# Batch 0's q and k in 128-token blocks, its first seven units one at a time, and half of the first MoE chunk in 512-token tiles

## The chip, the cores and the metric

The kernel runs on one core of one Trainium2 chip. The core has a matrix engine (TensorE, PE in the profile; its weight loads are listed apart as PEld), a vector engine (DVE), an activation engine (ACT), GpSimd (POOL) and SyncE (SP). SP, ACT and POOL also issue transfers to the core's 16 DMA engines. SBUF is the on-chip memory of 128 partitions; PSUM holds matmul results in eight banks of 128 x 512 float32. The metric is the device time of one execution in microseconds (us). Before the change the median of three runs is 310.25 us (309.75 to 310.46).

## The reference

Eight batches, eight heads, 576 tokens, head width 64. Attention has a sliding window of 128 tokens and a linear bias per head (ALiBi); its output, laid out as 4608 tokens by 512 features, goes through a two-matmul block with the activation h cos h.

```python
scores = scale * np.matmul(q, k.transpose(0, 1, 3, 2))
rel = pos[:, None] - pos[None, :]
mask = (rel >= 0) & (rel < window)                 # window = 128
scores = np.where(mask, scores + slopes * -abs(rel), -1e9)
attn = softmax(scores)                             # over keys
x = (attn @ v).transpose(0, 2, 1, 3).reshape(4608, 512)
h = x @ w_in                                       # 512 x 2048
out = (h * np.cos(h)) @ w_out                      # 2048 x 512
```

## The kernel before, in words

**Attention.** Queries of a batch come in five blocks of 128 tokens (the last has 64). The work is cut into units: unit (b, 0, 0) is block 0 with all eight heads; (b, qb, hh) for qb = 1 to 3 is a block with four heads; (b, 4, 0) is the 64-token tail with all heads. A unit computes `scores` (keys on the partitions, PE line 568, into two PSUM banks), an exponential on ACT over 128 x 1024 values (line 595), a multiplication by the mask on DVE (line 614; the first five units get bias and mask by a matmul into PSUM instead, line 582), the product with v (`pv`, PE lines 630 to 644; v has a column of ones for the sum), a division (`norm`, DVE lines 667 to 681), and a transposition of the result into the array `xT` (features on the partitions): by PE and a copy (`x_pe`, lines 702 to 731) or by DMA (`x_dma`).

**MoE.** Tokens go in nine chunks of 512. MoE1 makes 16 groups of 128 hidden features (fc 0 to 15) for a chunk, four matmuls each (one per 128 input features), then cos on ACT and a product on DVE into `gT`. From chunk 1 on a group is one PSUM bank of 128 features by 512 tokens (`moe1`, line 759, four matmuls of 512 columns). In chunk 0 `moe1_block` (line 784) fills a bank with four groups of features by 128 tokens, sixteen matmuls of 128 columns, so that it can start on tokens 0 to 127 before the later tokens exist. MoE2 (`moe2`, line 812) accumulates 16 matmuls of 512 columns per 128 tokens, copies the result and stores it.

**q and k.** Scores need q and k with head features on the partitions. Batches 2 to 7 are loaded in 128-token blocks into `qnat` and `knat` (`load_nat`, line 402) and transposed by DMA. Batches 0 and 1 are transposed by PE. They come as "rows": each partition takes several neighbouring tokens of one head, so a piece of memory read at once is 1 KB or more. Batch 0 is loaded in four such pieces (`PIECES`): tokens 0 to 127 (float32, by SP and ACT), 128 to 255, 256 to 511, and 512 to 575 (`qend`, `kend`); batch 1 in one. `qk_transposes` turns them: PE transposes of 128 x 64 into half of the partitions each (line 509, mode 2 of the planner; the first piece whole, line 504), then a copy out of PSUM by ACT or DVE (lines 524, 525) that also sorts the tokens. `tkeys` says which pieces a unit needs.

**Queues.** All loads but the first pieces go through POOL's queue in program order (lines 383, 391, 402, 423, 430): q and k pieces, v by 128-token block (`load_v`), w_in in five parts, w_out in four. The parts of w_in that chunk 0 waits for are called w0-1 (fc 0 and 1), w1-2 (fc 2 and 3), w2-4 (fc 4 to 7), w4-6 (fc 8 to 11), w6-8 (fc 12 to 15) here.

**The planner.** `Plan.op` records each operation with what it reads and writes, a cost and a priority; `Plan.schedule` orders them by a list schedule with those costs and emits the engines' programs with semaphore waits. On PE, operations of priority below 5 that can start at once go first; ties go by program order. All Sin activations of chunk 0 wait until the exponentials of the first seven units are done, since the activation table has to be switched. Until 8.3 us of plan time the planner fills PE's gaps with matmuls on zeros (line 945).

**Around the change.** `attention(every[0:7], -1)` runs units (0,0,0) to (0,3,1), which make tokens 0 to 511, in groups of two. Then comes chunk 0: `moe1_block` in the order (token block, group of four features) (0,0) (1,0) (2,0) (0,1) (1,1) (2,1) (3,0) (3,1), then groups 2 and 3 for the four token blocks; batch 1's row transposes come behind blocks 9 and 12. Chunk 0's MoE2 runs beside the attention of batch 1.

Of the kernel before, what the change touches and what calls it, by code (L numbers as in the profile page):

```python
# [6 lines left out]
ALU = mybir.AluOpType  # L7
ACTF = mybir.ActivationFunctionType
# [5 lines left out]
NBLK = 5  # L14
# [272 lines left out]
def bass_alibi_sliding__then__act_gcu_kernel(  # L287
# [8 lines left out]
    with ExitStack() as ctx:  # L296
# [13 lines left out]
        qE = {"q": sb("qend", [128, 2, 128]), "k": sb("kend", [128, 2, 128])}  # L310
# [51 lines left out]
        def piece_keys(which, b, n):  # L362
            return [("qB", which, i) for i in range(3)] if b else [("qB", which, n)]

        def load_qk(which, src, b, n=0):
            t0, rr, _ = PIECES[b][n]
            c0 = 64 * (t0 // 32)
            rows = bass.AP(src.tensor, src[b].offset + 64 * t0,
                           [[64 * rr, 32], [64 * S, H], [1, 64 * rr]])
            if b == 0 and n == 0:  # L370
# [8 lines left out]
                   r=[("qF", which)], w=piece_keys(which, b, n), occ={"act": 460, "dve": 330},  # L379
                   lat={"act": 560, "dve": 410}, pri=2)  # L380
                return
            o = qE[which][:, :, :] if t0 == 512 else qB[which][:, :, c0:c0 + 64 * rr]
            op("pool", [lambda e: e.dma_start(o, rows)],  # L383
               w=piece_keys(which, b, n), dma=f"ld{which}{n}", occ=750,
               lat={2: 600, 4: 800 if which == 'q' else 900,
                    8: 2600 if which == 'q' else 1300, 18: 2850}[rr])

        def load_v(b, order=range(NBLK), behind=()):
            for t in order:
# [6 lines left out]
                   occ=900, lat=7 * rows)  # L396

        def load_nat(which, src, b):
# [6 lines left out]
            op("pool", fns, w=[("nat", which)], dma=f"ldn{which}", occ=4400, lat=5500)  # L405
# [29 lines left out]
        def constants():  # L435
# [9 lines left out]
            for i, (edge, test) in enumerate([(-127.0, ALU.is_lt), (0.0, ALU.is_gt)]):  # L445
# [3 lines left out]
            op("dve", lambda e: e.tensor_tensor(dif[:, :, :], dif[:, :, :], off[:, :, :], ALU.add),  # L449
               r=[("off", 0), ("off", 1)], w=["dif"], occ=350, lat=430, pri=0)  # L450
            for i in range(2):
                op("dve", lambda e, i=i: e.memset(vp[i][:, :, :, 64:65], 1.0), w=[("vinit", i)],
                   pri=5 * i)
                op("dve", lambda e, i=i: e.memset(vp[i][64:128, 4, :, 0:64], 0.0),
                   w=[("vinit", i)], occ=270, pri=5 * i)
            for i in range(NP):
                op("dve", lambda e, i=i: e.memset(P[i][:, 1024:1088], 0.0), w=[("P", i)], occ=90)
            op("dve", lambda e: e.memset(halfpi[:, :], math.pi / 2.0), w=["halfpi"], occ=60)
# [28 lines left out]
        def qk_transposes(b, names, n, parts, banks):  # L487
# [8 lines left out]
            def dst(i):  # L496
                return ps[:, banks[i], :].bitcast(BF16)[:, 0:128 * (jobs[i][2] - jobs[i][1])]
# [479 lines left out]
```

## Time and profile before

| | |
|---|---|
| median of three runs | 310.25 us (309.75 to 310.46) |
| profiled execution, its own time | 310.24 us |
| span of the profile | 308.4 us |
| PE busy | 299.5 us (97%) |
| ACT busy | 200.3 us (65%) |
| DVE busy | 195.8 us (63%) |
| POOL busy | 97.0 us (31%) |
| granted PE clock | 1.00 in all windows |

The span lies inside the time of the execution; 1.84 us lie around it. An engine's busy time is the sum of its instructions; matmuls overlap in the records, so the pace of a group of matmuls is read from the distance between starts, or from the chain, which gives every stretch to one instruction only. A DMA row gives the time from the start of its issue to the landing of its last byte. KB are those written to SBUF (bf16), 1024 bytes each; GB/s of a window are bytes moved per time.

### The profile page before, as it was taken

How to read it: one execution, taken by the hardware profiler on the slowest of the kernel's cores; microseconds unless marked ns; L12 is line 12 of the kernel's file. 1: busy time of each engine (PE TensorE's matmuls, PEld its weight loads, DVE VectorE, ACT ScalarE, POOL GpSimd, SP SyncE). 2: the span in 40 equal slices, each digit the busy share in tenths (PEclk: the TensorE clock that was granted, in tenths of full speed). 3: DMA queues.
4: the chain of work that ended last, by engine and by line, in shares of the span. 5: the costliest groups of instructions: out<-in, count | busy, mean ns of one | idle time of the engine just before them, and what ended most of it. 6: DMA issues, size and time to landing. Idle time of an engine off the chain costs nothing.

```text
span 308.4 us, 6675 instructions
## 1 busy us (share of the span) xinstructions
PE 299.5 (97%) x2685; PEld 162.1 (53%) x2726; DVE 195.8 (63%) x409; ACT 200.3 (65%) x267; POOL 97.0 (31%) x122
## 2 busy tenths in 40 slices
PE   8889999999999999999999999999999999999996
PEld 6679755445554455445544554455445554444444
DVE  7688777574668566856785568656966588742000
ACT  6887973875478745873688378746964488752211
POOL 8997200455055505550347123900500000000000
PEclk9999999999999999999999999999999999999999
DMA  9999999999499958998699969995991420001112
GB/s 147 179 204 207 206 162 193 132 183 154 122 121 138 172 98 154 133 175 98 157 114 149 167 88 180 150 184 114 143 113 44 113 70 0 0 0 70 68 71 99
DMA packets 150333, 39.09 MB, mean 127 GB/s; under 512 B 138912, under 2 KB 145312, under 8 KB 150304
## 3 DMA queue, kind: packets, MB, share of 16 engines
q0 software_dynamic: 100688, 18.10, 79.5%
q1 hardware_dynamic: 49344, 20.33, 33.3%
q8 instruction: 21, 0.34, 0.5%
q10 hardware_dynamic: 272, 0.26, 0.3%
q14 instruction: 8, 0.07, 0.1%
HBM read 36.70 MB, written 9.44 MB: 150 GB/s over the span
## 4 chain that ended last, share of the span: by engine, by line
PE 90%; DMA 3%; POOL 2%; ACT 2%; issue 1%; DVE 1%; POOLq 0%; ACTq 0%
PE ps L812 38%; PE ps L759 36%; PE ps L568 5%; PE ps L784 4%; DMA w_inb<-in_moe_w_in_dram 3%; ACT p L595 2%; PE ps L642 2%; PE ps L644 2%; PE ps L630 1%; POOL vp L391 1%; PE ps L509 1%; DVE p L614 1%; PE ps L634 1%; POOL qrows L383 0%; PE ps L721 0%
## 5 line engine op out<-in xcount | busy, mean ns | idle before, releaser
L812 PE MATMUL ps<-w_outb,gT 128*128 128x512 bf16 (+2 forms) x566 | 132.1, 373 | 2.5 <-issue 1.3
L759 PE MATMUL ps<-xT,w_inb 128*128 128x512 bf16 x499 | 113.9, 379 | 0.7
L768 DVE TENSOR_TENSOR gT<-ps,cos 128x512 bf16<-128x512 f32 x128 | 85.1, 688 | 19.6 <-ACT cos L764 14.7
L764 ACT ACTIVATE cos<-ps,halfpi 128x512 f32<-128x512 f32 x128 | 84.6, 687 | 18.0 <-PE ps L759 13.9
L812 PEld LDWEIGHTS ps<-w_outb,gT 128*128 128x128 bf16 x592 | 53.4, 98 | 55.7 <-DVE ob L820 0.3
L595 ACT ACTIVATE p<-ps 128x1024 bf16<-128x1024 f32 x64 | 61.5, 1023 | 31.2 <-PE ps L568 31.0
L759 PEld LDWEIGHTS ps<-xT,w_inb 128*128 128x128 bf16 x512 | 49.0, 98 | 56.2 <-ACT p L595 0.6
L391 POOL DMA_DIRECT2D vp<-in_v_dram x40 | 33.7, 870 | 87.6 <-DMA xT<-xnat 67.4
L614 DVE TENSOR_TENSOR p<-p,emask 128x1024 bf16<-128x1024 bf16 x59 | 39.7, 684 | 27.8 <-ACT p L595 27.8
L819 ACT ACTIVATE ob<-ps 128x512 f32<-128x512 f32 (+2 forms) x21 | 12.1, 576 | 41.6 <-PE ps L812 35.2
L402 POOL DMA_DIRECT2D qnat<-in_q_dram x30 | 25.3, 877 | 22.5 <-DMA qt<-qnat 22.5
L402 POOL DMA_DIRECT2D knat<-in_k_dram x30 | 25.4, 884 | 12.3 <-DMA kt<-knat 9.8
L820 DVE COPY ob<-ps 128x512 f32<-128x512 f32 x16 | 11.0, 685 | 15.8 <-PE ps L812 15.7
L681 DVE TENSOR_TENSOR xnat<-ps,rec 128x256 bf16<-128x256 f32 x48 | 19.9, 421 | 1.3
L568 PE MATMUL ps<-qt,kt 64*128 64x128 bf16 (+1 forms) x576 | 19.4, 211 | 0.3 <-DVE qt L525 0.2
L642 PEld LDWEIGHTS ps<-vp,p 128*128 128x128 bf16 x192 | 14.2, 97 | 9.9 <-issue 6.4
L568 PEld LDWEIGHTS ps<-qt,kt 64*128 64x128 bf16 x576 | 14.5, 94 | 8.7 <-issue 3.5
L642 PE MATMUL ps<-vp,p 128*128 128x65 bf16 x192 | 17.4, 193 | 0.7 <-DVE xT L731 0.5
L644 PE MATMUL ps<-vp,p 128*128 128x65 bf16 x192 | 17.5, 193 | 0.0
L784 PE MATMUL ps<-xT,w_inb 128*128 128x128 bf16 x256 | 16.0, 219 | 0.6 <-DMA w_inb<-in_moe_w_in_dram 0.6
L784 PEld LDWEIGHTS ps<-xT,w_inb 128*128 128x128 bf16 x256 | 14.5, 98 | 1.3 <-DMA w_inb<-in_moe_w_in_dram 0.8
L644 PEld LDWEIGHTS ps<-vp,p 128*128 128x128 bf16 x192 | 13.2, 97 | 2.2
(66 smaller groups left out, 160.9 us busy)
## 6 DMA issues: line engine op xcount, KB each, us to landing
out_dram<-ob SPq DMA_DIRECT2D x35, 256.0 KB, 2.2
vp<-in_v_dram POOLq DMA_DIRECT2D x32, 128.0 KB, 7.1
qnat<-in_q_dram POOLq DMA_DIRECT2D x24, 128.0 KB, 6.5
knat<-in_k_dram POOLq DMA_DIRECT2D x24, 128.0 KB, 5.1
w_outb<-in_moe_w_out_dram POOLq DMA_DIRECT2D x4, 512.0 KB, 21.8
w_inb<-in_moe_w_in_dram POOLq DMA_DIRECT2D x3, 512.0 KB, 12.2
qrows<-in_q_dram POOLq DMA_DIRECT2D x1, 576.0 KB, 15.5
krows<-in_k_dram POOLq DMA_DIRECT2D x1, 576.0 KB, 17.5
```

Of the source, the lines that this page charges most:

```text
L391: op("pool", [lambda e, t=t, rows=rows: e.dma_start(vp[b % 2][0:rows, t, :, 0:64], v[b, :, 128 * t:128 * t + rows, :].rearrange("h p d -> ...
L402: fns.append(lambda e, t=t, rows=rows: e.dma_start(nat[which][0:rows, t, :, :], src[b, :, 128 * t:128 * t + rows, :].rearrange("h p d -> p ...
L568: ins = e.matmul(ps[:, banks[x], c0:c0 + n_], keys_ap(b, x, pr, kc), query_ap(b, x, pr, qb, n_), start=not acc, stop=stop)
L595: op("act", lambda e: e.activation(P[i][:, 0:1024], ps[:, banks[0]:banks[0] + 2, :].rearrange("p a b -> p (a b)"), ACTF.Exp, scale=0.125), ...
L614: op("dve", lambda e: e.tensor_tensor(p, p, m, ALU.mult), r=[("P", i), ("EM", 0), ("EM", 1)], w=[("P", i)], occ=600, lat=690, pri=1)
L642: e.matmul(o, P[i][:, c0:c0 + 128], V[:, qb - 1, h, 0:65], start=True, stop=False)
L644: ins = e.matmul(o, P[i][:, c0 + 128:c0 + 256], V[:, qb, h, 0:65], start=False, stop=True)
L759: op("pe", lambda e, kc=kc: e.matmul(ps[:, bank, :], w_in[:, kc, 128 * fc:128 * fc + 128], xT[:, kc, r0:r0 + CH], start=(kc == 0), stop=(k ...
L764: op("act", lambda e: e.activation(cosb[ci][:, :], ps[:, bank, :], ACTF.Sin, bias=halfpi[:, 0:1]), r=["halfpi"], w=[("B", bank), ("cos", c ...
L768: op("dve", lambda e: e.tensor_tensor(gT[gi][:, fc, :], ps[:, bank, :], cosb[ci][:, :], ALU.mult), r=[("cos", ci)], w=[("B", bank)] + [("g ...
L784: ins = e.matmul(ps[:, bank, 128 * i:128 * i + 128], w_in[:, kc, 128 * fc:128 * fc + 128], xT[:, kc, t0:t0 + 128], start=(kc == 0), stop=( ...
L812: op("pe", lambda e, t=t, fc=fc, bank=bank, j0=j0, j1=j1: e.matmul(ps[:, bank, 0:j1 - j0], gT[gi][:, fc, 128 * t:128 * t + 128], w_out[:, ...
```

## The change

Three things change, and with them some of the planner's numbers.

1. **q and k of batch 0 from token 128.** The pieces of rows go. Tokens 128 to 575 are loaded by `load_block` in 128-token blocks (t = 1 to 3; t = 4 has 64 tokens, its other rows are zeroed by DVE) into `qnat` and `knat`, in the layout of `load_nat`: one token per partition, 256 bytes read at once. `block_transposes` turns a block by four whole 128 x 128 transposes and one copy. A unit waits for its own blocks only (`tkeys`). The order of POOL's queue is written as a list: v3 moves behind w1-2, q3 and k3 lie behind w0-1. The first `load_nat` (batch 2) must wait until the blocks have been transposed. `qend` and `kend` go.
2. **The first seven units** are planned in groups of one, with the same two pairs of banks in turn.
3. **MoE1 of chunk 0, fc 8 to 15,** is done by `moe1` (four matmuls of 512 columns, all 512 tokens); fc 0 to 7 stay in blocks of 128 tokens. Batch 1's row transposes come behind tiles 10 and 13.

The initial values of the v buffers are set after the bias table's base is made; the planner's costs of a bias on DVE, of the first v block and of batch 1's rows are changed by some 50 to 500 ns.

```diff
-        PIECES = {0: [(0, 4, [(0, 4)]), (128, 4, [(0, 4)]), (256, 8, [(0, 4), (4, 8)]),
-                      (512, 2, [(0, 2)])],
-                  1: [(0, 18, [(0, 5), (5, 10), (10, 14), (14, 18)])]}
+        ROWS = [(4, [(0, 4)]), (18, [(0, 5), (5, 10), (10, 14), (14, 18)])]
...
+        def load_block(which, src, t):
+            rows = 128 if t < 4 else 64
+            op("pool", [lambda e: e.dma_start(
+                nat[which][0:rows, t, :, :],
+                src[0, :, 128 * t:128 * t + rows, :].rearrange("h p d -> p h d"))],
+               r=[("nend", which)] if t == 4 else [], w=[("nb", which, t)], dma=f"lb{which}{t}",
+               occ=900, lat=7 * rows)
...
-            op("pool", fns, w=[("nat", which)], dma=f"ldn{which}", occ=4400, lat=5500)
+            op("pool", fns, w=[("nat", which)] + [("nb", which, t) for t in range(1, NBLK)],
+               dma=f"ldn{which}", occ=4400, lat=5500)
...
+        def block_transposes(names, t, banks):
+            def f(e):
+                ins = None
+                for which, bank in zip(names, banks):
+                    for pr in range(NPAIR):
+                        ins = e.transpose(
+                            ps[:, bank, :].bitcast(BF16)[:, 128 * pr:128 * pr + 128],
+                            nat[which][:, t, 2 * pr:2 * pr + 2, :].rearrange("p h d -> p (h d)"),
+                            ident[:, :])
+                return ins
...
-            keys = [("tr", w_, b % 2) for w_ in ("q", "k")] + [("ktail", b % 2)]
-            if b < BPE:
-                lo, hi = 128 * max(0, qb - 1), 128 * qb + 128
-                keys += [("tr", w_, b % 2, t0 + j0) for w_ in ("q", "k")
-                         for t0, rr, groups in PIECES[b] if t0 < hi and t0 + 32 * rr > lo
-                         for j0, _ in groups]
+            keys = [("tr", w_, b % 2) for w_ in ("q", "k")]
+            if qb == 4 or b >= BPE:
+                keys += [("ktail", b % 2)]
+            if b == 0:
+                keys += [("tr", w_, 0, t) for w_ in ("q", "k") for t in range(max(0, qb - 1), qb + 1)]
...
-            sizes = ([[2] * 4] + GROUPS + [[], []])[phase + 1]
+            sizes = ([[1] * 7] + GROUPS + [[], []])[phase + 1]
...
-        load_qk("q", q, 0, 1)
-        load_qk("k", k, 0, 1)
-        load_v(0, [0])
-        load_qk("q", q, 0, 2)
-        load_qk("k", k, 0, 2)
-        load_v(0, [1])
-        load_w_in(0, 1)
-        load_v(0, [2, 3])
-        load_w_in(1, 2)
-        load_w_in(2, 4)
-        load_w_in(4, 6)
-        load_qk("q", q, 0, 3)
-        load_qk("k", k, 0, 3)
+        for x in "q1 k1 v0 q2 k2 v1 w0-1 q3 k3 v2 w1-2 v3 w2-4 w4-6 q4 k4 w6-8 qr kr v4".split():
...
+        for t in range(1, 4):
+            for which, bank in zip("qk", OB):
+                block_transposes([which], t, [bank])
...
-                    moe1_block(t, f4, seq[at % 6])
+                    if i >= 8:
+                        moe1(0, i, seq[at % 6])
+                    else:
+                        moe1_block(t, f4, seq[at % 6])
                     at += 1
-                    if i in (9, 12):
-                        qk_transposes(1, "q" if i == 9 else "k", 0, range(2),
-                                      UB + [seq[at % 6], seq[(at + 1) % 6]])
+                    if i in (10, 13):
+                        row_transposes(1, "q" if i == 10 else "k",
+                                       UB + [seq[at % 6], seq[(at + 1) % 6]])
```

More of the change, by code (lines that the diff above doesn't have):

```diff
@@ L395, in load_v @@
                    dma=f"ldv{b % 2}{t}",
-                   occ=900, lat=7 * rows)
+                   occ=900, lat=7 * rows + (500 if b == 0 and t == 0 else 0))
         def load_nat(which, src, b):
@@ new lines, in f @@
+                                qB[which][:, y, 64 * j:64 * j + 64], ident[:, :])
+                return ins
+            op("pe", f, r=[("rows", which, b), "ident"], w=[("B", x) for x in banks[:len(groups)]],
+               occ=58 * rr, lat=58 * rr + 200, mode=2 if b else 0, pri=3 if b else 2)
+            for i, (j0, j1) in enumerate(groups):
+                o = tr[which][b][:, :].rearrange("p (k t) -> p k t", k=NPAIR)[
+                    :, :, 0:32 * rr].rearrange("p k (s j) -> p k s j", j=rr)[:, :, :, j0:j1]
+                i_ = dst(i).rearrange("p (j s k) -> p k s j", j=j1 - j0, k=NPAIR)
+                copy_out(which, b, o, i_, 140 * (j1 - j0), [banks[i]], ("tr", which, b, j0))
```

136 lines of the change are left out of this document (66 added, 70 removed).

## The prediction

> **What bounds the kernel now.** I read the busy times by stretch first, then the chain that ended last, then PE's timeline up to 45 us, and last the DMA issues, narrowed until a single transfer stands in each answer. The windows (columns: stretch, its length, busy time and instructions of each engine, granted clock, DMA share, GB/s):
>
> ```profile
> 0.00:20.84 20.84, 17.69 (x272) 13.39 (x275) 14.46 (x53) 16.28 (x21) 20.03 (x31) 1.00 1.32 174
> 20.84:36.63 15.79, 15.40 (x315) 14.57 (x314) 13.45 (x22) 12.60 (x20) 9.80 (x12) 1.00 1.23 206
> 36.63:54.26 17.63, 17.36 (x188) 9.79 (x191) 12.39 (x32) 10.82 (x14) 0.90 (x2) 1.00 2.03 180
> 54.26:300.00 245.74, 243.16 (x1872) 120.96 (x1906) 155.49 (x304) 159.24 (x210) 66.26 (x79) 1.00 1.08 115
> ```
>
> From 20.84 to 300 us PE is busy for 275.92 of 279.16 us. Whatever the change does must show in two places: when PE's unbroken work begins, and how much of it there is. Ahead of 20.84 PE's 17.69 busy us hold zero matmuls, records that overlap, and waits for data; there the kernel is bound by arrivals. In the PE timeline and the chain this is seen directly:
>
> ```profile
> 17.33 0.84 PE L784 MATMUL ps<-xT,w_inb 128*128 128x128 bf16 x12 [0.63 <-DMA w_inb<-in_moe_w_in_dram]
> 19.47 0.20 PE L642 MATMUL ps<-vp,p 128*128 128x65 bf16 x1 [0.50 <-DVE xT L731]
> 19.73 0.39 PE L784 MATMUL ps<-xT,w_inb 128*128 128x128 bf16 x4
> 20.06 0.83 PE L784 MATMUL ps<-xT,w_inb 128*128 128x128 bf16 x12
> 20.84 2.62 PE L784 MATMUL ps<-xT,w_inb 128*128 128x128 bf16 x44
> ```
>
> The rows at 19.73 and 20.06 are block (2,0), tokens 256 to 383. PE had w1-2 from 17.33 on, but these tokens' xT was not there until about 19.7. From 20.84 on block (0,1) runs, the first that needs w2-4. When did w2-4 land? The issue (POOL timeline) and landing (DMA view):
>
> ```profile
> 8.61 2.27 POOL L423 DMA_DIRECT2D w_inb<-in_moe_w_in_dram  x3
> w_inb<-in_moe_w_in_dram POOLq DMA_DIRECT2D x1, 512.0 KB, 10.4
> ```
>
> Three issues in 2.27 us put the second at 9.37, so w2-4 landed at 19.77. It had 1.07 us in hand: before, the attention of batch 0 was late, not w2-4.
>
> **The change part by part.**
>
> *MoE1 fc 8 to 15 in 512-token tiles.* It takes away 128 matmuls of 128 columns and adds 32 of 512. Both paces are in the chain:
>
> ```profile
> 23.46 0.34 PE ps L509 x8
> 23.81 5.02 PE ps L784 x88
> 54.26 8.20 PE ps L759 x38
> 20.89 0.11 PE ps L721 x2
> ```
>
> 5.02/88 is 57.0 ns, 8.20/38 is 215.8 ns. 128 x 57.0 = 7.30 us against 32 x 215.8 = 6.91 us: 0.39 us less, inside PE's unbroken stretch, so I count it in full. ACT and DVE do the same number of cos and products on the same 128 x 512 shapes: nothing. The Trainium skill, "TensorE: Matmul & The Clock Gate", section Back-to-back issue gap, states for a sustained stream about 81 ns per matmul of 128 columns and 131 ns per one of 512. By that, 128 x 81 - 32 x 131 would save an estimated 6.2 us; the rows above disagree with both figures, and the sum goes by them.
>
> *Tail block t = 4.* Eight half transposes (0.34 us, the x8 row above) become eight whole ones; at 0.11 us for two (the L721 row, whole 128 x 128 transposes) that is 0.44 us: 0.10 us more, in the unbroken stretch too. The transposes of t = 1 to 3 change as well (48 halves to 24 whole), but lie ahead of 20.84, where PE waits for data: nothing; without that cover it would be a gain, 24 x 0.055 = 1.3 us for 48 x 0.032 to 0.042 (by rows of 36 and of 8 halves) = 1.5 to 2.0 us.
>
> *q and k in blocks: the wire.* Up to w2-4 POOL's queue carries the same bytes before and after; only the form of six times 128 KB changes, from rows of 1 KB and 2 KB read at once to 256 bytes. Windows in which one form prevails: 1 KB pieces of q and k at 4.8 to 5.6, 2 KB pieces at 6.4 to 8.4, batch 1's v in the blocks' layout at 40.5 to 44.5:
>
> ```profile
> 4.80:5.60 0.80, 0.80 (x5) 0.38 (x4) 0.80 (x9) 0.80 (x2) 0.80 (x2) 1.00 1.45 173
> 6.40:8.40 2.00, 1.89 (x36) 1.38 (x34) 1.26 (x4) 1.65 (x3) 2.00 (x3) 1.00 1.22 167
> 40.50:44.50 4.00, 3.95 (x50) 2.09 (x46) 2.66 (x7) 2.71 (x3) 0.00 (x0) 1.00 2.38 157
> ```
>
> 128 KB are 131 kB. Before: 262/173 + 524/167 = 4.65 us. After: 6 x 131/157 = 5.01 us. So w2-4 comes 0.36 us later, at 20.13. That is the low end. The high end comes from v blocks in the crowded start:
>
> ```profile
> 5.24 0.89 POOL L391 DMA_DIRECT2D vp<-in_v_dram  x1
> 6.87 1.78 POOL L391 DMA_DIRECT2D vp<-in_v_dram  x2
> vp<-in_v_dram POOLq DMA_DIRECT2D x1, 128.0 KB, 6.6
> vp<-in_v_dram POOLq DMA_DIRECT2D x1, 128.0 KB, 7.2
> vp<-in_v_dram POOLq DMA_DIRECT2D x1, 128.0 KB, 8.6
> ```
>
> v1 landed at 11.84, v2 at 14.07, v3 at 7.76 + 8.6 = 16.36. Between v1 and v3 lay w0-1 (262 kB, 1.27 us at the 206 GB/s of the second window) and two blocks: (4.52 - 1.27)/2 = 1.62 us a block. Six at that cost are 9.72 us, w2-4 5.1 us later. I take the low end, because it is a stretch of four us of mostly this layout. The Trainium skill's "DMA: Bandwidth & Descriptors", section Why small descriptors are slow, adds some 3 cycles to 32 bytes a cycle: 7 for 4 at 128 bytes, 19 for 16 at 512, 35 for 32 at 1 KB. By that the blocks would take an estimated 1.56 times the rows' 4.65 us, 2.6 us more; the three windows show 8%, so the trace does not bear this out there.
>
> *q and k in blocks: POOL's sequencer.* A row piece cost 0.70 to 0.84 us to issue, a block in this layout 0.89 (row above): six blocks for four pieces is 6 x 0.89 - 4 x 0.72 = 2.5 us more up to w2-4. But w2-4's issue at some 11.8 then still precedes its landing by over 8 us, and an uncrowded landing took 4.3 us from issue:
>
> ```profile
> vp<-in_v_dram POOLq DMA_DIRECT2D x1, 128.0 KB, 4.3
> 53.36 4.20 POOL L391 DMA_DIRECT2D vp<-in_v_dram  x5 [20.23 <-DMA xT<-xfirst]
> ```
>
> So the queue of transfers hides it. Later on, the new wait (batch 2's `load_nat` behind the transposes of t = 4, near 24 us on PE) holds up only the ten loads behind it, after which POOL sits idle for 20.23 us anyway: nothing. The zeroing of the tails is two small DVE memsets ahead of q4's issue; POOL behind it has transfers queued for 10 us: nothing. SP gets and loses nothing.
>
> *Units earlier.* A unit with qb = 2 now needs blocks 1 and 2 only, not tokens to 511. Before, k's 2 KB piece (issue 4.53, 6.4 us) landed at 10.9 and the third exponential group began at 13.48:
>
> ```profile
> 4.53 0.71 POOL L383 DMA_DIRECT2D krows<-in_k_dram  x1
> krows<-in_k_dram POOLq DMA_DIRECT2D x1, 256.0 KB, 6.4
> 6.13 0.76 POOL L423 DMA_DIRECT2D w_inb<-in_moe_w_in_dram  x1
> w_inb<-in_moe_w_in_dram POOLq DMA_DIRECT2D x1, 256.0 KB, 7.1
> 13.48 3.03 ACT L595 ACTIVATE p<-ps 128x1024 bf16<-128x1024 f32 x3 [0.88 <-PE ps L568]
> 16.74 1.02 ACT L595 ACTIVATE p<-ps 128x1024 bf16<-128x1024 f32 x1 [0.23 <-PE ps L568]
> ```
>
> After, 640 KB go up to and with k2 instead of 896, so it lands near 9.5, and units (0,2,0) and (0,2,1) go into the 0.88 us gap and ahead of it, some 1.5 us sooner: tokens 256 to 383 are in xT by about 18. Units (0,3,*) wait for k3, which has 1280 KB up to it, as w0-1 had before: 6.13 + 7.1 + 0.36 = 13.6. Transposes, a copy and scores take some 1.5 us more (k's old piece needed 13.48 - 10.93 = 2.55 us with twice the work), so the last exponential ends near 17.2 instead of 17.76 and the table switch for cos is 0.5 us sooner. That gains nothing on PE by itself: six PSUM banks take six blocks before a cos must have freed one.
>
> So blocks (0,0), (1,0), (2,0), of which half need only w0-1, can be done by about 19.2, 24 x 57 ns and two products with v behind w1-2's 17.3, and w2-4 is what is late next: PE's unbroken work begins at 20.2 rather than 20.84, 0.6 us sooner. Planning units singly changes only ties in the order: nothing by itself; its bounds are the two waits that such an order could add or save on PE, 0.50 and 0.63 us in the timeline above.
>
> *What follows.* If PE is 0.9 us ahead and transfers 0.36 to 0.46 late, the tightest later arrivals count:
>
> ```profile
> 12.97 0.70 POOL L383 DMA_DIRECT2D qrows<-in_q_dram  x1
> qrows<-in_q_dram POOLq DMA_DIRECT2D x1, 576.0 KB, 15.5
> 28.76 1.20 PE L509 MATMUL ps<-ident,qrows 128*64 128x128 bf16 x36
> 15.07 3.00 POOL L430 DMA_DIRECT2D w_outb<-in_moe_w_out_dram  x4
> w_outb<-in_moe_w_out_dram POOLq DMA_DIRECT2D x1, 512.0 KB, 22.7
> 40.80 2.33 PE L812 MATMUL ps<-w_outb,gT 128*128 128x512 bf16 x9
> ```
>
> Batch 1's q lands at 28.47 before, used at 28.76; after, at 28.9, and the transposes move one tile later: even. w_out's third part (16.57 + 22.7 = 39.3) is used at 40.80: 1.5 us of slack, of which 1.3 are used up. Nothing, but it ends there: no gain above about 1.1 us can be kept without waits at w_out.
>
> Sum: -0.39 + 0.10 - 0.6 = -0.9 us. Against the profiled execution's own 310.24 us (the runs' median is 310.25, no difference) that is **309.3 us**. Its own range is 308.8 to 309.8.
>
> **The rivals.**
>
> *Slower: the blocks clog the start.* If a block costs half way between 0.83 and 1.62 us, 1.22, six take 7.3 us, w2-4 lands 2.7 us later, at 22.4, and PE starts 1.6 us later than now: 310.24 + 1.6 - 0.3 = 311.5. For it: v2 to v3 took 2.3 us. Against: the 157 GB/s. It decides from 1.4 us of delay on w2-4 (1.07 in hand, 0.3 from PE's own savings), 1.0 us a block.
>
> *Only the tiles count.* w2-4 lands near 20.8; PE starts as before: 310.24 - 0.29 = 309.95.
>
> *More: the start is uncrowded.* The 2.28 us from v2 to v3 hold 1.45 us more than a block's 0.83. If that was an event of that moment and not the price of the layout, w2-4 lands at 20.13 - 1.45 = 18.7, and PE's unbroken work begins at 19.2, when the three blocks are done: 310.24 - 0.29 - 1.6 = 308.35. Against: the slack at w_out, which gives some of it back, and that PE's order is fixed by planned times.
>
> *The tiles at the skill's pace:* 310.24 - 0.5 - 6.2 is some 303.5; as a mechanism, PE's 128-column matmuls would have to be bound by their weight loads. PEld is 14.57 of 15.79 us busy in the second window, but the pace there is already 57 ns.
>
> **How the numbers follow.** Forecast 0.48, clogged start 0.27, tiles only 0.10, more 0.13, the skill's pace 0.02. A measurement of this kernel can tell about 0.2%, 0.62 us, from no change: faster means under 309.63, slower over 310.87. Of the forecast 0.40 lies under 309.63 and 0.08 within; of tiles only 0.03 and 0.07; of the clogged start 0.26 over and 0.01 within. Faster 0.58, same 0.16, slower 0.26. The range 308.3 to 311.5 leaves out the far half of the clogged start (0.13), and some 0.06 below.
>
> **What would show it.** Right: the first block on w2-4 starts at 20.0 to 20.4 after a wait on w_inb; L784 x128 and 32 more of L759; PE unbroken from there; L812 begins near 35.7. Wrong: w2-4 landing after 21.2; a wait of PE on w_out or v of batch 1 over 0.3 us between 35 and 45; the exponentials of units (0,2,*) no earlier than 13; the distance from chunk 0's MoE2 to the end changing by more than 0.3 us, since the planner reorders all that follows.

## The result, and the profile after

The changed kernel is slower: a median of 311.96 us (311.33 to 314.54, eight runs) against 310.05 us (309.49 to 310.99, eight runs) for the kernel before, a ratio of 1.0064 with a 95% interval of 1.0040 to 1.0087. The forecast was 309.3 us; the time lies outside the range of 308.3 to 311.5, on the side of the slower rival.

The profiled execution took 312.02 us with a span of 309.4 us; before it was 310.24 us with 308.4 us. So 1.0 of its 1.8 us lie inside the span, and 0.8 lie outside: 2.6 us around the span instead of 1.8. The windows of the changed kernel, cut at the same events as in the prediction (the first block on w2-4, here to 0.04 us, the start of chunk 0's MoE2, the start of chunk 1's MoE1):

```profile
0.00:20.48 20.48, 16.41 (x250) 12.31 (x251) 14.16 (x51) 15.35 (x20) 19.68 (x30) 1.00 1.57 161
20.48:36.89 16.41, 15.07 (x219) 10.66 (x220) 14.27 (x24) 13.83 (x23) 12.52 (x15) 1.00 1.29 204
36.89:54.31 17.42, 17.26 (x187) 9.68 (x190) 10.96 (x29) 11.14 (x17) 0.61 (x1) 1.00 1.94 177
54.31:300.00 245.69, 242.72 (x1869) 120.77 (x1904) 155.50 (x304) 159.07 (x211) 66.55 (x80) 1.00 1.12 116
```

In the second window PE is idle for 1.34 us (16.41 - 15.07); before, it was 0.39 (15.79 - 15.40). Some matmuls are missing from the record (2567 matmuls on 2609 weight loads, before 2685 on 2726), and a missing one looks like idle time. The weight loads show one missing at 30.7 in the changed kernel, and in both kernels the first matmul of MoE2: where all matmuls are recorded (e1 to e8 below), MoE2's first one begins with its second weight load, and that load lies at 36.68 here and at 36.42 before, where the first recorded matmuls are at 36.89 and 36.63. Without these, PE is idle for some 0.97 us, before for 0.18. What PE saves in chunk 0 it spends waiting in chunk 0. The places are in PE's timeline from 28 us on, first of the kernel before, then of the changed one (krows and qrows are the transposes of batch 1; L568 and L589 its first scores; L812 and L833 chunk 0's MoE2):

```profile
31.68 1.20 PE L509 MATMUL ps<-ident,krows 128*64 128x128 bf16 x36
32.80 2.85 PE L784 MATMUL ps<-xT,w_inb 128*128 128x128 bf16 x48
35.68 0.63 PE L568 MATMUL ps<-qt,kt 64*128 64x64 bf16 x24
36.63 3.18 PE L812 MATMUL ps<-w_outb,gT 128*128 128x512 bf16 x14 [0.32 <-DVE gT L794]
```

```profile
29.57 1.20 PE L516 MATMUL ps<-ident,qrows 128*64 128x128 bf16 x36
30.93 1.67 PE L780 MATMUL ps<-xT,w_inb 128*128 128x512 bf16 x7 [0.16 <-issue]
32.53 1.20 PE L516 MATMUL ps<-ident,krows 128*64 128x128 bf16 x36
33.66 1.47 PE L780 MATMUL ps<-xT,w_inb 128*128 128x512 bf16 x6
35.60 0.63 PE L589 MATMUL ps<-qt,kt 64*128 64x64 bf16 x24 [0.47 <-DVE kt L493]
36.89 2.75 PE L833 MATMUL ps<-w_outb,gT 128*128 128x512 bf16 x12 [0.66 <-DVE gT L789]
```

MoE1 does end sooner, at 33.66 + 1.47 = 35.13 instead of 32.80 + 2.85 = 35.65. But behind batch 1's k transposes, which begin 0.85 us later, only six matmuls of 512 columns (1.3 us) are left, where 48 of 128 columns (2.7 us) were left before. So PE now waits 0.47 us for the copies of k (kt) and another 0.45 us (0.66 less the missing matmul) for a product (gT), where it waited 0.1 us before (0.32 less the missing one). The product stands behind a cos, and the cos behind ACT's share of the copies; DVE was free 0.26 us earlier. The chain that ended last shows this path, first in the changed kernel, then before, where it is PE's work alone:

```profile
30.93 1.67 PE ps L780 x7
32.60 1.15 PE ps L516 x36
33.77 1.34 ACT kt L492 x2
35.11 0.57 ACT cos L785
35.71 0.70 DVE gT L789
```

```profile
31.68 1.20 PE ps L509 x36
32.87 2.79 PE ps L784 x48
35.68 0.63 PE ps L568 x24
```

The landing of the k rows is not on it. They land at 32.0 instead of 31.2, but the transposes begin at 32.53, directly behind PE's matmuls. The last transfer on this chain is v2's, at 15.96; from there to the end of the k transposes it is PE's work alone. The same stretch on DVE and ACT:

```profile
33.98 1.47 DVE L493 COPY kt<-ps 128x640 bf16<-128x640 bf16 x2
34.99 1.26 ACT L785 ACTIVATE cos<-ps,halfpi 128x512 f32<-128x512 f32 x2
35.71 1.29 DVE L789 TENSOR_TENSOR gT<-ps,cos 128x512 bf16<-128x512 f32 x2 [0.26 <-ACT cos L785]
```

MoE2 of chunk 0 begins 0.26 us later (36.68 instead of 36.42), and the rest of the span takes 272.67 us instead of 271.94. In that rest one wait of PE is named that the kernel before did not have, 0.38 us:

```profile
185.59 0.59 PE L780 MATMUL ps<-xT,w_inb 128*128 128x512 bf16 x2 [0.38 <-DMA xT<-xnat]
```

The landings, from the issue in POOL's timeline and the time to landing in the DMA view, first after, then before: w2-4 is the first of the two issues at 11.74 and lands at 11.74 + 8.7 = 20.4 (before 19.8), krows at 16.02 + 16.0 = 32.0 against 13.66 + 17.5 = 31.2:

```profile
11.74 1.57 POOL L422 DMA_DIRECT2D w_inb<-in_moe_w_in_dram  x2
w_inb<-in_moe_w_in_dram POOLq DMA_DIRECT2D x1, 512.0 KB, 8.7
16.02 0.71 POOL L374 DMA_DIRECT2D krows<-in_k_dram  x1
krows<-in_k_dram POOLq DMA_DIRECT2D x1, 576.0 KB, 16.0
```

```profile
13.66 0.71 POOL L383 DMA_DIRECT2D krows<-in_k_dram  x1
krows<-in_k_dram POOLq DMA_DIRECT2D x1, 576.0 KB, 17.5
```

ACT's timeline and one row of PE's show the attention of batch 0: the exponentials of tokens 256 to 383 come about as early as forecast (the second of the two at 11.43 and the one at 14.20, instead of 13.48 on), but those of tokens 384 to 511 begin at 17.04 and end at 18.98, and the table switch for cos is 1.2 us later than before (17.78):

```profile
11.43 2.04 ACT L616 ACTIVATE p<-ps 128x1024 bf16<-128x1024 f32 x2
14.20 1.02 ACT L616 ACTIVATE p<-ps 128x1024 bf16<-128x1024 f32 x1
17.04 1.94 ACT L616 ACTIVATE p<-ps 128x1024 bf16<-128x1024 f32 x2 [1.83 <-PE ps L589]
19.00 1.28 ACT L812 ACT_TABLE_LOAD   x1
```

```profile
16.01 0.20 PE L663 MATMUL ps<-vp,p 128*128 128x65 bf16 x1 [0.96 <-DMA vp<-in_v_dram]
```

PE's order holds a product with v2 ahead of those scores; v2 now lies behind q3 and k3 in POOL's queue and landed at 16.0 instead of 14.1.

Last, the part outside the span. The trace also lists transfers of kind instruction. Those on queue q8 carry 0.02 MB each, 20 to 22 in a run, and experiments f1 to f4, which change only PE's program, move them; so I read them as fetches of PE's program. In the DMA view of the 0.2 us from 311.15 on, 1.8 us behind the span's end, the changed kernel has one such record; behind the span of the kernel before there is none, its last one begins at 280.0:

```profile
DMA packets 1, 0.02 MB, mean 82 GB/s; under 512 B 0, under 2 KB 0, under 8 KB 0
q8 instruction: 1, 0.02, 33.3%
```

### The profile page after: what moved, and what is told of

It reads as the page before. It is cut to its first block, busy times and chain, and to the rows that moved or that the text cites. A ratio compares the mean times of both kernels' runs of the same rounds, so it can differ in the third digit from the quotient of the medians.

```text
span 309.4 us, 6443 instructions
## 1 busy us (share of the span) xinstructions
PE 298.3 (96%) x2567; PEld 157.3 (51%) x2609; DVE 194.9 (63%) x407; ACT 201.3 (65%) x271; POOL 99.4 (32%) x124
## 4 chain that ended last, share of the span: by engine, by line
PE 87%; DMA 4%; ACT 3%; POOL 3%; issue 1%; DVE 1%; POOLq 0%; ACTq 0%
PE ps L780 37%; PE ps L833 36%; PE ps L589 5%; ACT p L616 3%; PE ps L805 2%; DMA vp<-in_v_dram 2%; PE ps L663 2%; PE ps L665 2%; DMA xT<-xnat 1%; PE ps L651 1%; DVE p L635 1%; POOL qnat L380 1%; POOL knat L380 1%; PE ps L516 1%; PE ps L742 1%
## 5 line engine op out<-in xcount | busy, mean ns | idle before, releaser
L833 PE MATMUL ps<-w_outb,gT 128*128 128x512 bf16 (+2 forms) x566 | 131.8, 373 | 2.7 <-issue 1.1
L780 PE MATMUL ps<-xT,w_inb 128*128 128x512 bf16 x529 | 120.9, 379 | 1.3 <-DMA xT<-xnat 0.4
L789 DVE TENSOR_TENSOR gT<-ps,cos 128x512 bf16<-128x512 f32 x136 | 90.5, 688 | 21.1 <-ACT cos L785 16.2
L785 ACT ACTIVATE cos<-ps,halfpi 128x512 f32<-128x512 f32 x136 | 90.1, 688 | 19.3 <-PE ps L780 15.2
L780 PEld LDWEIGHTS ps<-xT,w_inb 128*128 128x128 bf16 x544 | 51.9, 98 | 59.8 <-ACT p L616 0.6
L833 PEld LDWEIGHTS ps<-w_outb,gT 128*128 128x128 bf16 x592 | 53.5, 98 | 55.9 <-issue 0.5
L840 ACT ACTIVATE ob<-ps 128x512 f32<-128x512 f32 (+2 forms) x23 | 13.2, 579 | 42.3 <-PE ps L833 42.3
L841 DVE COPY ob<-ps 128x512 f32<-128x512 f32 x14 | 9.6, 689 | 16.0 <-PE ps L833 15.9
L589 PE MATMUL ps<-qt,kt 64*128 64x128 bf16 (+1 forms) x576 | 19.3, 211 | 0.5 <-DVE kt L493 0.5
L589 PEld LDWEIGHTS ps<-qt,kt 64*128 64x128 bf16 x576 | 14.5, 94 | 9.4 <-DVE xnat L702 3.0
L663 PEld LDWEIGHTS ps<-vp,p 128*128 128x128 bf16 x192 | 14.0, 97 | 10.1 <-issue 6.7
L665 PEld LDWEIGHTS ps<-vp,p 128*128 128x128 bf16 x192 | 13.1, 97 | 2.1
L700 DVE RECIPROCAL rec<-ps 128x4 f32<-128x4 f32 x48 | 8.2, 176 | 6.7 <-PE ps L665 6.3
L651 PEld LDWEIGHTS ps<-vp,p 128*128 128x128 bf16 x128 | 7.2, 97 | 3.8 <-issue 2.3
```

Of the source, the lines that this page charges most:

```text
L589: ins = e.matmul(ps[:, banks[x], c0:c0 + n_], keys_ap(b, x, pr, kc), query_ap(b, x, pr, qb, n_), start=not acc, stop=stop)
L663: e.matmul(o, P[i][:, c0:c0 + 128], V[:, qb - 1, h, 0:65], start=True, stop=False)
L665: ins = e.matmul(o, P[i][:, c0 + 128:c0 + 256], V[:, qb, h, 0:65], start=False, stop=True)
L780: op("pe", lambda e, kc=kc: e.matmul(ps[:, bank, :], w_in[:, kc, 128 * fc:128 * fc + 128], xT[:, kc, r0:r0 + CH], start=(kc == 0), stop=(k ...
L785: op("act", lambda e: e.activation(cosb[ci][:, :], ps[:, bank, :], ACTF.Sin, bias=halfpi[:, 0:1]), r=["halfpi"], w=[("B", bank), ("cos", c ...
L789: op("dve", lambda e: e.tensor_tensor(gT[gi][:, fc, :], ps[:, bank, :], cosb[ci][:, :], ALU.mult), r=[("cos", ci)], w=[("B", bank)] + [("g ...
```

## The experiments

Theories: W, PE's wait for v2 (0.96 us) eats the gain; K, the landing of batch 1's k rows and what hangs on it sets chunk 0's end, so that savings of PE before it don't count; PE-bound, the prediction's own; R, the later chunks, planned anew, run in a worse order; T, the tiles themselves cost; and from the sixth run on F, the fetch of the last piece of PE's program lies behind the span. None of the kernels leaves out part of the computation. "Around" is a run's time less its span; for the kernel before it was 1.83 to 1.94 us in all of its runs beside the experiments. Each session has its own runs of the kernel before: medians 310.14, 310.15, 310.06 and 310.00 us, spans 308.1 to 308.25.

The last column is the second weight load of chunk 0's MoE2, so that missing matmul records play no part; for the kernel before it is 36.42. It is one execution each, and f2's was the slowest of its twelve.

| run | us | ratio, 95% interval | span | around | chunk 0's MoE2 from (profile) |
|---|---|---|---|---|---|
| after | 311.96 | 1.0064 [1.0040, 1.0087] | 309.35 | 2.10 to 3.54 | 36.68 |
| e1 v2 first | 311.32 | 1.0034 [1.0020, 1.0048] | 308.9 | 1.76 to 3.10 | 36.62 |
| e2 before, tiles | 310.82 | 1.0020 [1.0007, 1.0033] | 308.6 | 2.12 to 2.31 | 36.56 |
| e3 before, extra load | 310.79 | 1.0018 [1.0007, 1.0028] | 308.9 | 1.85 to 1.93 | 37.31 |
| e4 after, no tiles | 310.70 | 1.0017 [1.0009, 1.0026] | 308.55 | 2.08 to 2.17 | 36.61 |
| e5 after again | 311.93 | 1.0052 [1.0034, 1.0069] | 308.95 | 2.09 to 3.53 | 36.25 |
| e6 e2, 232 ns planned | 310.41 | 1.0003 [0.9994, 1.0012] | 308.55 | 1.85 to 1.91 | 37.01 |
| e7 after, 232 ns planned | 311.33 | 1.0044 [1.0027, 1.0060] | 308.9 | 2.10 to 3.51 | 35.37 |
| e8 after, no tiles, pairs | 312.20 | 1.0058 [1.0043, 1.0073] | 310.05 | 2.13 to 2.22 | 37.03 |
| f1 after, 18 matmuls more | 311.49 | 1.0048 [1.0029, 1.0066] | 309.35 | 2.12 to 2.26 | 36.26 |
| f2 after, 20 matmuls fewer | 310.88 | 1.0026 [1.0012, 1.0040] | 308.75 | 2.09 to 2.17 | 37.32 |
| f3 before, 11 matmuls more | 310.72 | 1.0024 [1.0009, 1.0039] | 308.45 | 1.85 to 3.32 | 36.60 |
| f4 before, 31 matmuls more | 310.48 | 1.0013 [1.0001, 1.0024] | 308.6 | 1.85 to 2.49 | 36.14 |
| g1 f1, rows early | 310.99 | 1.0032 [1.0018, 1.0045] | 309.2 | 1.79 to 1.94 | 36.58 |
| g2 before, rows early | 310.02 | 0.9999 [0.9989, 1.0010] | 308.2 | 1.78 to 1.88 | 36.25 |
| g3 g2 with tiles | 310.89 | 1.0028 [1.0017, 1.0038] | 308.7 | 2.14 to 2.29 | 36.16 |

**e1: v2 ahead of q3 and k3.**

```diff
-"q1 k1 v0 q2 k2 v1 w0-1 q3 k3 v2 w1-2 v3 w2-4 ..."   # after
+"q1 k1 v0 q2 k2 v1 w0-1 v2 q3 k3 w1-2 v3 w2-4 ..."
```

> The changed kernel with v2 put back ahead of q3 and k3 in POOL's queue. Theory W (the wait of PE on v2, with the scores of the last two units queued behind it, is what ate the gain): no PE wait on vp over 0.3 us near 16 us; the exponentials of the seven units end by 18.0 instead of 18.98; chunk 0's MoE2 begins near 36.2 instead of 36.89; the time is about 0.7 us under the changed kernel's. Theory K (the landing of batch 1's k rows sets the end of chunk 0, whatever PE has done before): the exponentials end sooner too, but k's rows land at 32.0 as before and MoE2 begins at 36.7 to 36.9; the time is within 0.3 us of the changed kernel's.

The wait on v2 is gone and the exponentials end at 18.2 instead of 19.0, but MoE2 begins at 36.62, as in the changed kernel (36.68). PE is done with the blocks ahead of the tail's transposes at 22.8 instead of 24.2 and then waits for the tail block of k, a wait that the changed kernel's profile does not have:

```profile
24.07 0.40 PE L534 MATMUL ps<-ident,qnat 128*128 128x128 bf16 x4 [1.24 <-DMA knat<-in_k_dram]
```

The kernel takes 1.0034 times as long as before, and its median span is 0.05 us (beside e5) to 0.45 us (beside the first measurement) shorter than the changed kernel's. W is at most a small part.

**e2: the tiles alone in the kernel before.**

```diff
-                    moe1_block(t, f4, seq[at % 6])
+                    if i >= 8:
+                        moe1(0, i, seq[at % 6])
+                    else:
+                        moe1_block(t, f4, seq[at % 6])
```

> The kernel before with nothing but MoE1 fc 8 to 15 of chunk 0 in 512-token tiles. PE-bound (the prediction's own step): 0.39 us less, MoE2 of chunk 0 begins at 36.25 instead of 36.63, ratio 0.9987. Theory K: MoE1's matmuls end 0.4 us sooner, but PE then waits that much longer behind the copies of batch 1's k; MoE2 begins at 36.5 to 36.7, ratio 0.9995 to 1.000.

0.7 us slower instead of 0.4 faster, about half of it in the span and half around it. MoE2 begins 0.14 us later. PE's saving stands as a wait for gT right ahead of batch 1's scores, 0.56 us where the kernel before had 0.1 behind them:

```profile
35.96 0.63 PE L568 MATMUL ps<-qt,kt 64*128 64x64 bf16 x24 [0.56 <-DVE gT L768]
```

**e3: batch 1's rows later.** One load of 128 KB in the blocks' layout, into a tile that nothing reads, goes ahead of batch 1's rows.

```diff
+        op("pool", [lambda e: e.dma_start(spare[:, :, :],
+            q[0, :, 128:256, :].rearrange("h p d -> p h d"))], w=["spare"], dma="ldx", occ=900, lat=0)
         load_qk("q", q, 1)
```

> The kernel before with one more 128-KB load, in the blocks' layout and into a tile that nobody reads, ahead of batch 1's rows in POOL's queue. Theory K: k's rows land 0.8 us later, at 32.0, and MoE2 of chunk 0 begins 0.5 to 0.8 us later, at 37.1 to 37.4; ratio 1.0015 to 1.0025. PE-bound: the landing is covered, MoE2 begins at 36.6 to 36.8, ratio 1.000 to 1.0005.

The k rows land at 32.46 instead of 31.21 and MoE2 begins 0.89 us later; the profile's span is 0.94 us longer, the median span 0.65: what delays chunk 0's end is passed on in full. The k transposes began 0.47 us behind the landing before; here they begin 0.1 us behind it, so this much later the rows do bind. In PE's timeline the lateness shows as a wait for the q rows:

```profile
29.68 1.20 PE L510 MATMUL ps<-ident,qrows 128*64 128x128 bf16 x36 [0.70 <-DMA qrows<-in_q_dram]
32.56 1.20 PE L510 MATMUL ps<-ident,krows 128*64 128x128 bf16 x36
37.31 1.02 PE L813 MATMUL ps<-w_outb,gT 128*128 128x512 bf16 x4
```

**e4: the changed kernel without the tiles.**

```diff
-                    if i >= 8:
+                    if i >= 16:
                         moe1(0, i, seq[at % 6])
```

> The changed kernel with all of chunk 0's MoE1 in blocks of 128 tokens, as before the change (blocks and single units stay). PE-bound: 0.39 us more than the changed kernel, MoE2 begins at 37.3. Theory K: PE's extra 0.4 us falls into the 1.3 us in which it waits behind k's copies at the end of chunk 0; MoE2 begins at 36.9 to 37.0 and the time is that of the changed kernel within 0.2 us.

1.3 us faster than the changed kernel, although PE has 0.39 us more to do. The span is 0.4 to 0.8 us shorter (beside e5 and the first measurement), the time around it 2.1 to 2.2 in every run. The k rows land at 31.85, their transposes begin at 32.56, and MoE2 begins at 36.61, 0.07 us sooner than in the changed kernel and 0.19 later than before the change.

**e5: the changed kernel again.**

> The changed kernel, unaltered, beside the variants on one chip, since the kernel with blocks for all of chunk 0 (e4) was 1.2 us faster than it and differs only in chunk 0. If the difference belongs to the kernel: ratio 1.005 to 1.007, MoE2 of chunk 0 from 36.8 to 37.0. If much of it was one chip or the single execution: ratio 1.003 to 1.004 and MoE2 near 36.6.

The same, 311.93 us; its profile has a span of 308.5 us with 2.98 around it. MoE2 begins at 36.25, 0.43 us sooner than in the first profile: w2-4 had landed 0.41 sooner, and the waits behind MoE1 are the same 0.9 us. The rest of the span takes 272.22, without the 0.38 us at xT, which is thus not a fixed part.

**e6 and e7: tiles planned dearer.** The planner's cost of a 512-column matmul in chunk 0 goes from 216 to 232 ns, so that PE's order behind chunk 0 in e6 (e2 otherwise) is nearly that of the kernel before; e7 is the changed kernel with the same cost.

```diff
-                   occ=216, lat=379, pri=5)
+                   occ=232 if c == 0 else 216, lat=379, pri=5)
```

> The kernel before with the 512-token tiles as in e2, but with a planned cost of 232 ns for each of chunk 0's 512-column matmuls, so that the plan has the old times; PE's order behind chunk 0 is then that of the kernel before. Theory R (what e2 lost, it lost because the planner ordered all later chunks anew): MoE2 of chunk 0 begins at 36.5 to 36.6 as in e2, the stretch from there to the last MoE2 is 236.9 to 237.1 as before, ratio 0.9990 to 1.0002. Theory T (the tiles themselves cost, for example by their later k transposes): ratio 1.002 as in e2.

> The changed kernel with the same planned cost of 232 ns for chunk 0's 512-column matmuls. Batch 1's k transposes then stand at least as far ahead of the end of chunk 0 as with blocks (e4). Theory K with R: MoE2 of chunk 0 begins at 36.5 to 36.7 instead of 36.89 and the time is that of e4, ratio 1.001 to 1.0025. Theory T: it stays at the changed kernel's ratio, 1.005 to 1.007.

e6 is 0.4 us below e2, and the same as the kernel before. But the spans of e2 and e6 are alike (308.6 and 308.55); the difference is in the time around. So it is no proof of R as I had put it. It shows that the tiles, with the order kept, gain nothing; in its profile PE waits 0.71 us for the tail block of k (kend). e7 has MoE2 at 35.37, 1.3 us sooner than the changed kernel. Of this, 1.0 us is an earlier start in that execution (v2 landed at 14.9 instead of 16.0, w2-4 at 19.45 instead of 20.48). In PE's order, eight matmuls are left behind the k transposes instead of six, and PE waits 0.46 us behind MoE1 instead of 0.92. Then PE runs into w_out, and the median span is that of e5:

```profile
35.37 1.46 PE L833 MATMUL ps<-w_outb,gT 128*128 128x512 bf16 x6 [0.33 <-DVE gT L789]
37.49 1.90 PE L833 MATMUL ps<-w_outb,gT 128*128 128x512 bf16 x8 [0.67 <-DMA w_outb<-in_moe_w_out_dram]
```

**e8: the blocks alone, units in pairs.**

```diff
-            sizes = ([[1] * 7] + GROUPS + [[], []])[phase + 1]
+            sizes = ([[2] * 4] + GROUPS + [[], []])[phase + 1]
-                    if i >= 8:
+                    if i >= 16:
```

> The changed kernel without its tiles and without its single units: q and k in 128-token blocks, units in groups of two, all of chunk 0 in blocks. If single units matter only for ties: the time of e4, ratio 1.001 to 1.0025, exponentials of the units (0,3,*) within 0.3 us of e4's. If pairs put the scores of a pair ahead of the products with v, the last exponentials end 0.5 us or more sooner, but MoE2 of chunk 0 still begins at 36.5 to 36.8 (theory K).

1.5 us slower than e4, which differs in the grouping alone, all of it in the span (310.05 against 308.55). The list of PE's waits from 10 to 120 us (us in total, times, longest) has 0.9 us on w_in and 0.7 on exponentials, where e4's has 0.9 on blocks of q and k:

```profile
PE ps L805 <- DMA w_inb<-in_moe_w_in_dram: 0.9, 1, 0.9
PE ps L651 <- ACT p L616: 0.4, 1, 0.4
PE ps L663 <- ACT p L616: 0.3, 1, 0.3
```

**f1 to f4: the length of PE's program.** The matmuls on zeros that fill PE's first microseconds are made more or fewer; nothing else changes. f1 and f2 are the changed kernel, f3 and f4 the kernel before.

```diff
+        warm, extra = [], {19: 18}        # f3: {19: 11}; f4: {19: 20, 31: 11}
+
+        def filler(e):
+            for _ in range(1 + extra.get(len(warm), 0)):
+                ins = e.matmul(ps[:, UB[1], 0:128], zeros[:, :], zeros[:, :],
+                               start=True, stop=True)
+            warm.append(1)
+            return ins
```

```diff
-                   fill=(900, 8300))
+                   fill=(4000, 8300))      # f2
```

> The changed kernel with 18 more warm-up matmuls (36 more instructions in TensorE's program, all in its idle time ahead of the first q and k, 3.3 to 5.5 us). In the trace of the changed kernel the last 16-KB piece of code on the instruction queue (q8) is fetched 1.85 us behind the end of the span; in the kernel before it is fetched at 280.0, in e2_b_tiles (whose TensorE program is 41 instructions longer than the changed kernel's) at 301.1. Theory F (the time around the span, 2.1 to 3.5 us, is the wait for that piece, because the program's end lies just past the boundary of a piece): the last fetch moves to 295-306 us, inside the span; the time around the span is 2.1-2.3 in every run, and the total falls by 0.6-1.0 to 311.0-311.3, with the span as before the edit (308.9-309.3). Theory C (the time around the span comes from what the change does: blocks and tiles together): 311.9 again, 2.1 to 3.5 around the span.

> The changed kernel without its first 20 warm-up matmuls (40 instructions fewer in TensorE's program). Theory F: the program's end lies before the boundary, so the 21st piece is never fetched: the last fetch on the instruction queue is at about 278, the time around the span is 1.75-2.2 and does not scatter, total 310.7-311.3 if the missing warm-up costs nothing at the start. Theory C: 311.9 again.

> The kernel before with 11 more warm-up matmuls (22 more instructions in TensorE's program, in its idle time from 3.3 to 4.6 us): its program's end then lies at the same place in a 16-KB piece as the changed kernel's. Nothing else is changed. Theory F: a fetch on the instruction queue appears behind the end of the span, the time around the span rises from 1.9 to 2.1-3.5 and scatters, and the total rises by 0.5-1.3 to 310.6-311.4 although the span stays at 308.2-308.4. Theory C: 310.1, 1.9 around the span.

> The control of f3: the kernel before with 31 more warm-up matmuls (62 more instructions), which puts the program's end as far past the boundary as that of e2_b_tiles. Theory F: the last fetch is at 295-306 us, inside the span; 1.9-2.2 around the span, total 310.1-310.5, below f3 although it has 20 warm-up matmuls more. If more warm-up matmuls cost something by themselves: above f3.

F holds in all four for the time around. In f1 the last record of q8 moves from 311.2 to 301.1, inside the span, and the time around is 2.12 to 2.26 in every run. In f2 there is no 21st record, the last begins at 283.0, and it is 2.09 to 2.17. In f3, eleven matmuls on zeros at 3.3 us make the kernel before 0.66 us slower, with a record at 309.8 behind a span of 308.5 and times around of 1.85 to 3.32; twenty more of them (f4) bring the time around back to 1.85 to 1.95 in eleven of twelve runs, though the total stays 0.42 us above the kernel before. The DMA view of f3 from 309.7 to 309.9:

```profile
DMA packets 1, 0.02 MB, mean 82 GB/s; under 512 B 0, under 2 KB 0, under 8 KB 0
q8 instruction: 1, 0.02, 32.5%
```

The size of the saving was less clear in the totals than around the span: f1 was forecast at 311.0 to 311.3 and came out at 311.49, since its median span was 309.35; its interval and that of e5 overlap widely.

**g1 to g3: batch 1's rows ahead of the last quarter of w_in.** g1 is f1 with the list below, g2 the kernel before with the same move, g3 is e6 with it.

```diff
-"... w2-4 w4-6 q4 k4 w6-8 qr kr v4"
+"... w2-4 w4-6 q4 k4 qr kr w6-8 v4"
```

> The changed kernel with f1's 18 extra warm-up matmuls and batch 1's q and k rows queued ahead of the last quarter of w_in instead of behind it. Theory K (chunk 0's end is set by the landing of batch 1's k rows): k rows land at 29.1-29.6 instead of 31.9, w6-8 at 31.9-32.3 instead of 26.1; TensorE then waits some 0.3-0.6 for w6-8 and the sixteen matmuls on it take 3.45, so MoE2 of chunk 0 begins at 35.5-36.1 (f1 36.47, after 36.89), its 4.6-4.9 us distance to the k rows is gone, and the span falls by 0.3-0.8 from f1's (308.9 profiled, 309.35 median). If the k rows were not the bound: MoE2 of chunk 0 at 36.4-36.9, the same span.

> The kernel before with the same two loads moved ahead of the last quarter of w_in. K: k rows land at about 28.6; MoE1 in 128-token tiles then ends no sooner than w6-8 allows (31.2-31.5 plus 64 matmuls at 57 ns, 3.65) and TensorE's own pace (35.66 before): MoE2 of chunk 0 at 35.9-36.5 against 36.64, total 309.6-310.2 against 310.1.

> g2 with the 512-token tiles (planned at 232 ns in chunk 0, as in e6). If the k rows were what swallowed the tiles' saving: MoE2 of chunk 0 another 0.2-0.4 sooner than in g2, total 0.1-0.4 below g2's. If the tiles save nothing in any place: the same as g2 or above it, as e6 is beside the kernel before.

In g1 the k rows land at 29.1, as expected, but MoE2 begins at 36.58 and the span gains nothing. So the landing of the k rows is not the bound, which is the second of the two forecasts. w6-8 now lands last, at 31.5, and the k transposes wait for a PSUM bank:

```profile
31.01 1.20 PE L516 MATMUL ps<-ident,krows 128*64 128x128 bf16 x36 [1.18 <-DVE gT L789]
32.14 3.63 PE L780 MATMUL ps<-xT,w_inb 128*128 128x512 bf16 x15
36.58 3.40 PE L833 MATMUL ps<-w_outb,gT 128*128 128x512 bf16 x15 [0.25 <-DVE gT L789]
```

The transposes write a bank that a product (gT) has to free first. g2 equals the kernel before. g3 starts MoE2 0.09 us sooner than g2, and both profiles begin chunk 1's MoE1 at 52.90; g3's rest from there is 0.28 us longer, and 0.37 us more lie around the span. No kernel tried beats the one before.

## Why the prediction was wrong

It forecast -0.9 us and the measurement is +1.9 us. By its own steps:

- **The tiles, "0.39 us less, inside PE's unbroken stretch, so I count it in full".** This step failed. The paces were right, and MoE1 ended 0.5 us sooner. The counting failed: PE's matmuls are not what ends chunk 0 any more. PE waits 0.92 us for kt and gT in the changed kernel and 0.56 in e2, where 0.1 stood before. The stretch looked unbroken in the kernel before because the copies of k, the cos and the product were done within 0.1 us of PE's own work. And e6, whose waits behind MoE1 are as short as before, gains nothing either, with 0.71 us of waiting for kend in its profile.
- **"The transposes move one tile later: even".** This looked at the landing of the q rows, and left out what follows the k transposes: the copies, a cos and a product. In the changed kernel these are no longer hidden. The wait behind MoE1 goes with the matmuls that are left behind the k transposes: 0.8 to 0.9 us where they are worth 1.3 us (after, e5, f1, f2), 0.3 to 0.5 with 1.7 to 1.8 (e1, e4, e7), about 0.1 with 2.6 to 2.7 (e6 and the kernel before). e2 (0.56 with 2.2) and e8 (0.32 with 2.5) lie above this line, and no run moves the transposes alone, so the size of this part is argued from the profiles.
- **Theory K is not borne out as to the landing of the k rows.** MoE2 begins 4.4 to 4.9 us behind the k rows in the eight profiles where these land at 31.6 us or later (after, e1, e3, e4, e5, e6, f1, f2). But the k transposes begin 0.1 us behind the landing only in e3, 0.2 in e6 and 0.4 to 0.9 in the other six, and the chain that ended last holds this landing in none of the profiles. Its last transfer ahead of MoE2 differs: v2 (after, e5), w2-4 (f2, e8), the q rows (f1, e3), the tail block of k (e1, e4, e6). So arrivals still bound chunk 0 behind 20.84 us in many executions, by tenths, and which of them it is changes from one to the next.
- **The start, "0.6 us sooner".** The first block on w2-4 came 0.3 us sooner in the profiled run, at 20.5 against 20.8 (20.1 and 19.8 in e5 and f1). w2-4 landed 0.7 later instead of 0.36, just before it was needed, but PE waited for it only in f2 (0.77 us). In the changed kernel's profile the chain comes from v2 instead, whose delay the prediction did not count; that the block began as w2-4 landed is chance. Such landings vary from one execution to the next: in the nine profiles with blocks w2-4 lands at 19.3 to 21.3 (median 19.8), in the eight without at 18.8 to 19.9 (19.6). Where nothing else moves the k rows, they land at 31.1 to 32.8 (31.8) in eight with blocks and at 30.9 to 32.2 (31.3) in five without. So the medians are 0.2 and 0.5 us later, which does not contradict the 0.36 to 0.46 us of the wire. The half of it that I put on the units (0,3,*) went the other way: exponentials ending at 18.98 instead of 17.2, by v2 behind q3 and k3 in POOL's queue with its product ahead of their scores in PE's order. e1 shows that this cost little.
- **"Planning units singly changes only ties in the order: nothing by itself."** Beside the blocks it is worth 1.5 us (e8 against e4), more than its bounds of 0.50 and 0.63. No run has single units in the kernel before.
- **The later chunks.** The list of signs named a change of over 0.3 us from chunk 0's MoE2 to the end, and gave it no price. It came: 271.94 before, 272.67 after. Five profiles with the old order (before, e3, e6, f3, f4) have 271.9 to 272.2, four with the new (after, e5, f1, f2) 272.2 to 272.7, so about 0.5 us between the medians. Which waits make it up is not settled; the largest named one (0.38 us at xT) is not in e5.
- **Outside the span.** The sum was "made against its own time", and took the 1.84 us around the span for fixed. They were 2.1 to 3.5 in the 14 runs of the changed kernel, median 3.0. That is about half of the loss. Some 0.9 of these 1.1 us go when 18 matmuls on zeros are added or 20 taken away (f1, f2: 2.1 to 2.3), so in this part blocks and tiles count by how many instructions they leave in PE's program. The Trainium skill's "Runtime: NRT & Kernel Launch", section Instruction fetch mechanics, says that an engine's instructions come in blocks of 256, fetched ahead by the engine's own queue, mostly hidden. The records on q8 agree with the blocks (0.02 MB each). Counted that way, with a matmul for every weight load, the recorded instructions of PE end 173 into a block in the kernel before and 156 in f2, with no further fetch; 194 to 196 in the four kernels with the wide scatter (after, e1, e7, f3); and 232 to 237 in f1, f4, e2 and e6, where the last block is fetched at about 301. "Mostly hidden" does not hold in the middle group. Four profiles have a record behind the span, 1.23 (f3), 1.76 (e7), 1.85 (after) and 2.29 us (e5) behind its end, and their times around are 2.08, 2.77, 2.62 and 2.98, each 0.7 to 1.0 us more. The profile of e1 has no such record, and 1.99 around. What delays the fetch differently in each execution is not shown.

Together: no gain up to chunk 0's end, some 0.5 us in the later chunks and some 1.1 around the span; the rest of the 1.9 us is not placed.

The clogged start, the rival for slower, did not come: w2-4 was 0.7 us late, not 2.7, and PE took it up sooner than before, not later.

## What to carry to other kernels

Before a saving on the busy engine is counted in full, follow every arrival up to the end of that stage, also those that are on time by a few tenths now, and what the other engines still have to do behind its last work: a stretch without waits can have two bounds at once, and then shortening one only shows the other. That two events keep their distance does not make one the cause of the other; look whether the chain that ended last goes through it. Where a few tenths of a per cent matter, look at the time around the span and at the records of the instruction queue behind its end, since adding or removing a few matmuls anywhere can move the end of a program across a block. To price a part of a change, vary that, and compare spans and the time around them apart.

## What was not expected of the hardware

- Eleven matmuls on zeros in idle time cost 0.66 us (f3: 1.0024, interval 1.0009 to 1.0039), 31 of them 0.4 (f4: 1.0013, 1.0001 to 1.0024). Only the eleven put a fetch of PE's program behind the end of the span.
- The time around the span has two further levels, 1.8 to 1.9 us (before, e3, e6, g1, g2 and all but one run of f4) and 2.1 to 2.3 us (e2, e4, e8, f1, f2, g3), with no record that tells them apart. e2 and e6 have the same number of matmuls and differ only in order. This stays open.
